# More zero products in TensorE's opening waits and a new order of the first 640 steps of a fused attention and gated-MLP kernel

## The chip, the cores and the metric

One core of one Trainium2 chip. The metric is the device time of one execution in microseconds, as the median of several runs. A profile is one further execution; its span runs from the first to the last instruction of the program.

## What is computed

Eight batches of attention with eight heads of 576 positions and 64 channels, in a causal window of 128 positions with a linear bias for each head; then, on the joined heads (576 by 512), a gated MLP whose gate mixes positions.

```python
scores = scale * q @ k.T + bias          # masked to 0 <= i - j < 128
x = softmax(scores) @ v                  # heads side by side: 576 x 512
h = gelu(x @ w_in)                       # 576 x 1024
u, v = h[:, :512], h[:, 512:]
v_n = (v - mean(v)) / sqrt(var(v) + 1e-6) * g_ln
gated = u * (w_sg @ v_n + b_sg[:, None])
out = x + gated @ w_out
```

All inputs and outputs are float32.

## The kernel before, in words

Attention is done for pairs of heads: 32 pairs, numbered 0 to 31, four to a batch. The MLP follows for each batch, its products split into a high and a low part (three products for one). The weights come from memory as float32 in 64-bit words and are split on the chip, which is work of the opening alone: the eight blocks of w_in must be split ahead of the first u product.

The kernel is a list of named steps. Each step belongs to one engine and issues a few instructions. The text `ORDER` (from L1150) holds all steps in one written-out order, and the loop at L1232 issues them so; each engine runs its own steps strictly in that order, and the engines are held together by semaphores alone. A step is named by a letter and a number. The steps of pair n (`Pair.STEPS`, table `add_pair`):

- q, L: loads of q and k, and of v, on SyncE's queue (SP). Each engine's DMA steps stand in one queue, so a load that waits for a free buffer holds up those behind it.
- a, c (and * for both): the scores on TensorE (PE), L278, 20 and 16 products.
- A, B, C, G: bias, mask and row minima on VectorE (DVE), L302 and L295. They free the PSUM banks of the scores.
- e, E, f, F, j: the exponentials on ScalarE (ACT), L311.
- R: the inverse of the sums, DVE, L322 and L323.
- s, S, r: the scaling, on ACT (L329) and GpSimd (POOL, L334).
- t, T, z: transposes on PE, L347 and L360; X, Y: the masked copies on DVE, L356; P: a copy on ACT, L363.
- V: the weighted values on PE, L384 (36 products) and L388 (4); x, p on ACT and 2 on DVE (L396) join them. So "20", "21", "22", "23" are step 2 of pairs 0 to 3.
- h on ACT and l on POOL: the high and low parts of the pair's output (L401, L218).

Pairs 0, 1, 3, 2 come first in this order. The splitting of weight block k is i (load, L181), d (ACT, L192 and L194), b (DVE, L196), o (DVE, L198), + (POOL, L218), H (ACT, L203) and - (DVE, L208, for odd k; POOL, L218, for even k). wl, wH, w- do it for the mixing weights. The four staging buffers of i and wl are shared: each later load waits until + of an earlier block has given one free.

Of the first batch's MLP, w and v on PE (L607 to L609) build the v half pair by pair: w20 is block 2 of positions from pair 0, and v0t closes block t with pair 2, the last. u000 is the first product group of the u half. vg is the gelu of v on ACT (L786).

A step Wi issues so many products of a zeroed tile, named `spare`, as the list `IDLE` says, into a PSUM bank of the named pool (L1139); nobody reads them. It needs the zeroed tile (L90) and a free buffer of that pool: two pools, ps_s and ps_a, have two one-bank buffers each, and ps_m has two of two banks.

Of the kernel before, what the change touches and what calls it, by code (L numbers as in the profile page):

```python
# [21 lines left out]
def attention_gmlp(  # L22
# [1123 lines left out]
    for b in range(B):  # L1146
# [14 lines left out]
        nv30h P4 bH nt0c vn03 b- vn02 V4 nt0h x4 d8 p4 uc01 tn0 b11 o11 b8 24 o8 y020 y021 *7 +11 ug0 A7 +8 B7 y000
        y001 H11 j7 H8 Us0 C7 G7 -11 -8 Us1 gm02 gm00 F7 E7 f7 e7 q9 q6 L6 *6 A6 R7 gh00 gh02 h4 B6 C6 e6 q8 L7 s7
        y010 y011 t7 S7 gl02 r7 T7 y030 G6 gm01 X7 F6 E6 f6 j6 R6 gl00 s6 S6 Y7 y031 z7 gm03 gh01 h5 P7 V7 p7 gh03
        gl01 t6 T6 X6 Y6 Oa0 x7 gl03 r6 O00 z6 27 oa00 Us2 l4 l5 P6 h7 V6 p6 x6 Us3 26 O01 h6 l6 l7 *8 oa01 A8 B8 C8
        Us4 G8 u100 u101 e8 *9 E8 f8 j8 F8 R8 A9 B9 u110 s8 S8 r8 t8 C9 k4 k7 Uh1 uc10 E9 j9 f9 e9 k5 k6 Ul1 X8 G9
# [105 lines left out]
```

## Time and profile before

| what | value |
|---|---|
| median of 3 runs | 577.91 us (577.79 to 578.27) |
| span of the profiled execution | 577.4 us |
| median less span | 0.5 us |
| instructions | 14654 |
| PE busy | 560.8 us, 97% of the span |
| DVE busy | 473.8 us, 82% |
| ACT busy | 378.6 us, 66% |
| POOL busy | 308.0 us, 53% |

For the profiled execution only its span is shown, so sums are made against 577.4 us, and 0.5 us is added for the median of the runs. The page gives one execution: the busy time of each engine, the chain of work that ended last, and the costliest groups of instructions. The trace behind it gives windows of time, timelines and waits. The granted clock is TensorE's alone, as a share of 2.4 GHz; ahead of its first record (at 14.2 us here) the windows show 1.00, and the products' durations have to tell.

### The profile page before, as it was taken

To read this page: it belongs to the slowest core of one execution; us is meant where nothing else is said; L and a number is where in the kernel's file an instruction comes from. 1 tells how busy PE (TensorE), PEld (TensorE's weight loads), DVE (VectorE), ACT (ScalarE), POOL (GpSimd) and SP (SyncE) were. 2 spreads that over 40 slices of the span, in tenths; PEclk is the share of its full clock that TensorE was granted. 3 is DMA by queue.
4 is the path that set the end of the run, shared out by engine and by line. 5 is a ranking of instruction groups with operands and counts; after the bars stand their busy time and mean duration, and the time that the engine had idled before them with its cause. 6 is when DMAs were issued, how large, how long until landed. Compare 5 with 4: busy or idle time off the path is not lost.

```text
span 577.4 us, 14654 instructions
## 1 busy us (share of the span) xinstructions
PE 560.8 (97%) x5495; PEld 512.7 (89%) x5495; DVE 473.8 (82%) x1324; ACT 378.6 (66%) x1063; POOL 308.0 (53%) x365
## 2 busy tenths in 40 slices
PE   5889999999999999999999999999999999999997
PEld 4667899998899799997999998998989999998997
DVE  7989998799989868899788987878897988666646
ACT  7988997466853867467776576746695667833422
POOL 3676646530436543575447753496347653576325
PEclk9989999999999999999999999999999999999999
DMA  8675213216403413454260465135332606012502
GB/s 297 190 235 199 72 45 121 69 46 243 167 37 125 156 37 99 146 192 129 60 212 10 140 204 173 43 103 168 130 120 65 214 2 197 2 35 96 171 1 82
DMA packets 43561, 69.78 MB, mean 121 GB/s; under 512 B 3554, under 2 KB 31202, under 8 KB 43492
## 3 DMA queue, kind: packets, MB, share of 16 engines
q1 hardware_dynamic: 43492, 68.86, 36.7%
q8 instruction: 43, 0.70, 0.5%
q14 instruction: 26, 0.21, 0.1%
HBM read 56.27 MB, written 12.58 MB: 119 GB/s over the span
## 4 chain that ended last, share of the span: by engine, by line
PE 90%; DVE 5%; DMA 2%; ACT 1%; issue 1%; POOL 0%; SPq 0%; DVEq 0%; ACTq 0%
PE ps_m L607 13%; PE ps_m L1059 13%; PE ps_m L609 12%; PE ps_m L608 12%; PE ps_m L905 12%; PE ps_a L347 5%; PE ps_s L384 4%; PE ps_s L278 4%; PE ps_a L278 4%; PE ps_m L384 3%; DMA qk<-qkT 2%; PE ps_m L941 2%; PE ps_m L940 1%; DVE px L356 1%; DVE e L295 1%; PE ps_m L796 1%
## 5 line engine op out<-in xcount | busy, mean ns | idle before, releaser
L334 POOL TENSOR_TENSOR e<-e,rr 128x256 f32<-128x256 f32 (+2 forms) x116 | 80.7, 718 | 97.0 <-DVE rr L323 84.9
L311 ACT ACTIVATE e<-e,stats 128x128 f32<-128x128 f32 (+1 forms) x288 | 110.6, 386 | 17.7 <-DVE stats L295 17.1
L224 POOL TENSOR_TENSOR region<-u,region 128x288 fp32r<-128x288 f32 (+1 forms) x78 | 77.7, 1016 | 44.7 <-ACT region L1006 16.2
L356 DVE TENSOR_TENSOR px<-ps_a,m_both 128x1024 f32<-128x1024 f32 x64 | 77.4, 1216 | 5.9 <-PE ps_a L347 5.4
L607 PE MATMUL ps_m<-ws,region 128*128 128x288 f32 x256 | 78.2, 306 | 0.0
L609 PE MATMUL ps_m<-ws,region 128*128 128x288 f32 x256 | 75.7, 296 | 0.0
L608 PE MATMUL ps_m<-ws,region 128*128 128x288 f32 x256 | 75.6, 295 | 0.0
L730 POOL TENSOR_TENSOR rs<-rs,mhalf 128x1 f32<-128x1 f32 (+1 forms) x40 | 30.2, 756 | 57.4 <-DVE rs L727 57.2
L218 POOL TENSOR_TENSOR xs<-xf,xs 128x288 fp32r<-128x288 f32 (+1 forms) x48 | 49.9, 1060 | 13.8 <-ACT xs L401 13.8
L311 ACT ACTIVATION_READ_ACCUMULATOR e<-e,stats 128x1 f32 x288 | 54.4, 189 | 0.0
L1006 ACT ACTIVATE region<-u 128x576 fp32r<-128x576 f32 x35 | 23.7, 684 | 43.4 <-PE ps_m L608 17.4
L607 PEld LDWEIGHTS ps_m<-ws,region 128*128 128x128 f32 x256 | 48.3, 189 | 1.5 <-issue 0.8
L608 PEld LDWEIGHTS ps_m<-ws,region 128*128 128x128 f32 x256 | 48.2, 188 | 0.1
L609 PEld LDWEIGHTS ps_m<-ws,region 128*128 128x128 f32 x256 | 48.1, 188 | 0.1
L607 PE MATMUL ps_m<-wi,xs 128*128 128x512 f32 x112 | 46.9, 418 | 0.1
L1066 DVE TENSOR_TENSOR xf<-ps_m,xf 128x576 f32<-128x576 f32 x48 | 35.7, 750 | 10.9 <-PE ps_m L1059 10.1
L609 PE MATMUL ps_m<-wi,xs 128*128 128x512 f32 x112 | 44.3, 395 | 0.0
L608 PE MATMUL ps_m<-wi,xs 128*128 128x512 f32 x112 | 44.2, 395 | 0.0
L946 DVE TENSOR_TENSOR u<-ps_m,u 128x576 f32<-128x576 f32 x32 | 24.0, 752 | 18.7 <-PE ps_m L941 11.5
L347 PE MATMUL ps_a<-ident,e 128*128 128x128 f32 x256 | 38.0, 275 | 1.0 <-DVE px L356 1.0
L295 DVE CUSTOM_DVE_ANT_0 e<-ps_s,bias 128x128 f32<-128x128 f32 (+1 forms) x140 | 34.9, 287 | 2.5
L278 PE MATMUL ps_s<-qk 64*64 64x192 f32 (+2 forms) x576 | 31.5, 333 | 5.3 <-DMA qk<-qkT 4.9
(217 smaller groups left out, 1600.9 us busy)
## 6 DMA issues: line engine op xcount, KB each, us to landing
qk<-qkT SPq DMA_DIRECT2D x32, 576.0 KB, 4.7
sum<-store SPq DMA_DIRECT2D x36, 512.0 KB, 4.8
outT<-xf SPq DMA_DIRECT2D x31, 288.0 KB, 3.0
vt<-v_in SPq DMA_DIRECT2D x32, 256.0 KB, 4.1
wst<-w_in SPq DMA_DIRECT2D x8, 512.0 KB, 4.8
store<-sum SPq DMA_DIRECT2D x6, 512.0 KB, 2.7
vt<-v_in SPq DMA_DIRECT2D x64, 32.0 KB, 4.2
wst<-w_out SPq DMA_DIRECT2D x4, 512.0 KB, 3.6
```

Of the source, the lines that this page charges most:

```text
L218: (engine or nc.gpsimd).tensor_tensor(out[:, cs], a[:, cs], b[:, cs], op)
L224: nc.gpsimd.tensor_tensor(out[:, fs], a[:, fs], b[:, fs], ALU.subtract)
L278: return lambda: nc.tensor.matmul(banks[half][to, c:c + k1 - k0], qk[js, 0, q0:q0 + R], qk[js, 1, k0:k1], start=True, stop=True)
L311: nc.scalar.activation(x, x, AF.Exp, bias=self.nm[0:n, i:i + 1], scale=-1.0, accum_out=self.sm[0:n, i:i + 1])
L334: nc.gpsimd.tensor_tensor(x[:, z:z + step, :], y[:, z:z + step, :], self.rr[0:n, i + z:i + z + min(k, step)].rearrange("p (m o) -> p m o", ...
L347: burst([lambda t=t: nc.tensor.transpose(cv[:, t // 2, t % 2], self.pr[j][:, t, :].rearrange("p (h c) -> p h c", h=2), ident[:, j * R:j * ...
L356: nc.vector.tensor_tensor(xv, cv, mv, ALU.mult)
L607: nc.tensor.matmul(dst, ah, bh, start=(first and i == 0), stop=False)
L608: nc.tensor.matmul(dst, ah, bl, start=False, stop=False)
L609: nc.tensor.matmul(dst, al, bh, start=False, stop=(last and i == n - 1))
L905: nc.tensor.matmul(dst, left(n, g, c)[:, ms], right(n, h, c), start=first and c == 0 and k == 0, stop=c == 1 and k == 2, skip_group_check= ...
L1059: nc.tensor.matmul(dst, p, q, start=first and f == 0 and k == 0, stop=f == 1 and k == 2, skip_group_check=True)
```

## The change

The list of the zero products becomes longer (24 entries with 85 products, where there were 12 with 51), and the steps of all engines up to some 640 of 2003 stand in a new order. No step is added or taken out but W steps, and from step gh15 on, in the MLP of the second batch, the order is the same. Two of the W steps, W7 and W11, now stand ahead of the first scores a0. On PE the last W step is now W22, ahead of t3; before, four stood behind t3 (W10 and W6, then W7 ahead of z3, and W1 ahead of u000).

```diff
-    IDLE = [(12, "ps_a"), (4, "ps_a"), (4, "ps_s"), (4, "ps_s"), (4, "ps_a"), (4, "ps_m"), (4, "ps_m"), (3, "ps_m"), (4, "ps_m"), (4, "ps_m"), (2, "ps_m"), (2, "ps_m")]
+    IDLE = [(4, "ps_m"), (4, "ps_m"), (5, "ps_m"), (1, "ps_m"), (4, "ps_a"), (4, "ps_a"), (4, "ps_a"), (4, "ps_a"), (4, "ps_a"), (5, "ps_a"), (2, "ps_m"), (1, "ps_m"), (4, "ps_m"), (4, "ps_m"), (2, "ps_m"), (3, "ps_m"), (4, "ps_m"), (3, "ps_m"), (3, "ps_a"), (4, "ps_a"), (5, "ps_a"), (5, "ps_s"), (4, "ps_s"), (2, "ps_s")]
...
-        q0 i2 d2 i1 q1 a0 c0 A0 a1 i0 B0 C0 G0 b2 c1 e0 d1 E0 F0 j0 f0 d0 b1 o2 o1 +2 A1 R0 B1 C1 b0 o0 G1 L0 i5 q3 i3
-        j1 H2 s0 E1 e1 f1 r0 F1 d3 S0 +0 +1 -2 W0 t0 X0 W5 T0 Y0 W2 W4 z0 R1 b3 o3 P0 r1 V0 z1 H0 p0 s1 H1 x0 a3 A3 B3
-        t1 20 X1 c3 C3 G3 -0 +3 S1 T1 W9 wl2 wH2 P1 w-2 i6 q2 d5 d6 H3 h0 wl3 L1 i7 q5 L2 F3 j3 e3 E3 f3 d7 a2 b5 b6
-        o5 +5 l0 Y1 A2 B2 R3 o6 -3 -1 b7 W11 W8 W3 V1 s3 w20 t3 W10 W6 x1 p1 j2 e2 21 h1 +6 S3 X3 c2 l1 w30 T3 W7 w00
-        w21 E2 wH3 C2 f2 G2 F2 r3 z3 w-3 H6 P3 Y3 R2 s2 -6 o7 S2 +7 L3 i9 i4 gb i10 V3 x3 23 p3 k1 H5 r2 h3 w01 t2 w10
-        T2 X2 Y2 l3 w31 w11 z2 d4 d10 P2 V2 x2 H7 p2 b4 o4 b10 o10 22 +4 +10 w13 w33 *5 A5 B5 C5 G5 w03 w23 h2 H4 d9
-        l2 v03 v02 v00 v01 W1 e5 j5 vg03 H10 vg02 vg00 vg01 -5 b9 o9 -7 -4 nv30b nv00b nv10b -10 +9 nv00p u000 u030
...
+        W7 q0 W11 i2 d2 a0 c0 A0 B0 W21 C0 G0 e0 b2 q1 i1 a1 A1 j0 E0 c1 L0 f0 B1 F0 R0 d1 i0 W6 i3 j1 W9 s0 W13 S0 r0
+        o2 +2 b1 o1 +1 W4 q2 q3 d0 C1 W8 W20 f1 G1 F1 t0 W5 W0 X0 T0 Y0 E1 W15 b0 o0 +0 W12 W1 z0 e1 R1 P0 i5 W10 d3 b3
+        o3 W23 i6 V0 W16 r1 z1 a3 L1 x0 wl2 +3 20 p0 W17 A3 B3 W3 s1 t1 H0 S1 gb X1 c3 -0 C3 G3 T1 h0 l0 W2 i7 L2 d6 d5
+        b5 o5 Y1 b6 W14 a2 A2 B2 w20 w30 e3 wH2 E3 w-2 H1 wl3 -1 W18 P1 d7 j3 V1 f3 w00 W19 b7 o7 F3 R3 e2 j2 x1 o6 W22
+        21 s3 p1 t3 X3 +5 c2 r3 E2 +7 C2 S3 T3 h1 G2 Y3 +6 w10 wH3 H2 z3 l1 w11 f2 F2 P3 -2 R2 q5 H3 -3 L3 V3 w-3 s2 S2
+        w01 t2 i10 x3 23 i4 H6 -6 r2 p3 w31 h3 i9 X2 l3 T2 Y2 d10 b10 d4 w21 z2 P2 d9 V2 tl o10 w33 b4 x2 o4 +4 b9 22 H7
+        -7 p2 h2 l2 +10 H4 H5 w23 k1 *5 L5 w03 A5 o9 v03 B5 v00 e5 C5 v02 vg00 -4 wl0 vg03 G5 vg02 k2 w13 v01 +9 -5 u000
...
```

## Rows read from the trace of the kernel before

**Rows 1.** The page: busy time of each engine, and the chain that ended last.

```profile
PE 560.8 (97%) x5495; PEld 512.7 (89%) x5495; DVE 473.8 (82%) x1324; ACT 378.6 (66%) x1063; POOL 308.0 (53%) x365
...
PE 90%; DVE 5%; DMA 2%; ACT 1%; issue 1%; POOL 0%; SPq 0%; DVEq 0%; ACTq 0%
```

**Rows 2.** Windows: stretch, length, each engine's busy time (instructions), granted clock, DMA share, GB/s.

```profile
6.50:31.21 24.71, 18.89 (x204) 14.28 (x196) 22.84 (x99) 23.98 (x87) 14.03 (x11) 1.00 0.80 256
...
28.40:31.26 2.86, 1.41 (x9) 0.98 (x8) 2.68 (x14) 2.82 (x15) 2.66 (x2) 1.00 0.88 305
...
31.29:34.71 3.42, 3.42 (x41) 2.96 (x42) 3.39 (x6) 2.83 (x9) 2.54 (x2) 0.50 0.36 108
...
56.98:160.00 103.02, 103.02 (x1065) 93.34 (x1069) 93.36 (x278) 76.47 (x220) 47.10 (x48) 1.00 0.32 107
```

The engines stand in the order PE, PEld (weight loads), DVE, ACT, POOL.

**Rows 3.** Timeline of PE in the opening: start, duration, line, operation, tiles, shape, count [idle before].

```profile
4.86 1.56 PE L278 MATMUL ps_s<-qk 64*64 64x128 f32 x20 [4.86 <-DMA qk<-qkT]
...
9.64 1.56 PE L278 MATMUL ps_m<-qk 64*64 64x128 f32 x20 [1.94 <-DMA qk<-qkT]
...
12.41 2.66 PE L1139 MATMUL ps_a<-spare 128*128 128x288 f32 x12
...
21.00 0.88 PE L278 MATMUL ps_s<-qk 64*64 64x128 f32 x20
...
31.26 2.88 PE L384 MATMUL ps_s<-px,vt 64*64 64x128 f32 x36
...
34.28 0.68 PE L607 MATMUL ps_m<-wi,xs 128*128 128x512 f32 x1
...
35.27 0.60 PE L347 MATMUL ps_a<-ident,e 128*128 128x128 f32 x4
35.62 1.36 PE L1139 MATMUL ps_m<-spare 128*128 128x288 f32 x6
...
41.30 1.57 PE L384 MATMUL ps_s<-px,vt 64*64 64x128 f32 x36
...
55.85 0.69 PE L1139 MATMUL ps_a<-spare 128*128 128x288 f32 x4
56.98 0.40 PE L607 MATMUL ps_m<-xs,wi 128*128 128x288 f32 x1 [0.43 <-ACT xf L786]
```

**Rows 4.** Timeline of DVE in the opening, with the same columns.

```profile
18.68 1.03 DVE L322 TENSOR_SCALAR rr<-stats 128x9 f32<-128x9 f32 x1
...
21.97 0.30 DVE L302 COPY_PREDICATED ps_s<-sel,ps_s 128x128 f32<-128x128 uint8 x1 [1.00 <-PE ps_s L278]
...
31.12 0.17 DVE L322 TENSOR_SCALAR rr<-stats 128x9 f32<-128x9 f32 x1
...
34.31 1.26 DVE L196 TENSOR_SCALAR tmp<-tmp 128x512 int32<-128x512 int32 x1
...
37.83 0.30 DVE L302 COPY_PREDICATED ps_s<-sel,ps_s 128x128 f32<-128x128 uint8 x1 [0.54 <-PE ps_s L278]
...
43.41 0.69 DVE L396 TENSOR_TENSOR xf<-ps_s,xf 128x512 f32<-128x512 f32 x1 [1.97 <-ACT xf L393]
...
46.62 0.42 DVE L196 TENSOR_SCALAR tmp<-tmp 128x512 int32<-128x512 int32 x1
47.07 0.69 DVE L198 SCALAR_TENSOR_TENSOR tmp<-wst,tmp 128x512 int32<-128x512 int32 x1
...
48.14 1.67 DVE L198 SCALAR_TENSOR_TENSOR tmp<-wst,tmp 128x512 int32<-128x512 int32 x1
49.73 0.68 DVE L396 TENSOR_TENSOR xf<-ps_s,xf 128x512 f32<-128x512 f32 x1
```

**Rows 5.** Timeline of POOL in the opening, with the same columns.

```profile
33.80 1.49 POOL L334 TENSOR_TENSOR e<-e,rr 128x512 f32<-128x512 f32 x1
...
47.90 1.36 POOL L218 TENSOR_TENSOR tmp<-tmp,wst 128x512 int32<-128x512 int32 x1 [1.41 <-ACT p L363]
```

More of the change, by code (lines that the diff above doesn't have):

```diff
@@ L1161, in attention_gmlp @@
[L1161 to L1165, printed above, removed]
@@ new lines, in attention_gmlp @@
+        nt1c D00 r9 nt1p u110 q11 V8 x8 p8 nt1h t9 X9 28 u120 Us9 T9 Y9 u111 tn1 z9 P9 u121 Uh3 L9 uc12 Ul3 ks0 ks1 ks2
+        ks3 uc11 V9 p9 x9 ks4 29 kh0 kl0 ks5 ug1 ks6 kh1 kl1 O03 oa03 q10 O02 oa02 D02 *10 A10 B10 C10 G10 E10 f10 e10
+        j10 F10 v10 *11 A11 vg10 L10 v11 R10 r10 s10 vg11 t10 B11 C11 nv01b nv01c nv01p nv01h nv11b nv11p nv11c v12 vn10
+        nv11h X10 vn11 vg12 v13 ya100 ya101 vg13 kh2 nv21b nv21c S10 q12 nv21p nv21h T10 E11 G11 ya110 z10 nv31b nv31p
+        Y10 P10 ya111 nv31c nv31h vn12 vn13 kl2 ks7 ks8 V10 y110 f11 y111 gm11 j11 e11 ks9 x10 q13 D03 F11 kh3 R11 s11
@@ new lines, in attention_gmlp @@
+        y100 y101 gm10 kl3 kd0 y120 y121 y130 h9 t11 gh11 gl11 gt11 210 h8 p10 y131 l9 kd1 gm12 gh15 X11 gm13 O11 S11
+        gl15 r11 gt12 T11 z11 O15 h10 gh12 gh16 gh13 P11 Y11 oa11 gl12 V11 x11 p11 gl16 gt13 O16 211 gh17 oa15 oa16 gt14
+        *13 gl13 O13 gl17 ut25 oa13 O17 A13 oa17 O12 B13 oa12 h11 gh14 gl14 l8 O14 C13 oa14 G13 l10 l11 E13 k10 uh25 k9
+        k11 k8 v20 v21 vg20 ul25 vg21 j13 ut26 ut27 nv02b nv02c nv02p nv02h nv12b nv12p nv12c nv12h vn20 vn21 *12 tt2
+        U21 kd2 lu21 lu22 q14 lu20 L12 D11 D10 q15 L13 tj2 U25 uh27 f13 uh26 e13 ue21 A12 B12 ut24 ul27 ul26 U26 F13
@@ new lines, in attention_gmlp @@
+        ue25 U23 uh24 E12 ue26 U27 C12 ue23 G12 R13 e12 f12 j12 F12 U22 ue27 R12 ul24 U24 ue22 r12 s12 z12 t12 S12 tg2
+        nt2b nt2p s13 X12 nt2c ue24 v22 T12 Y12 v23 vg22 nv22b P12 nt2h tn2 vg23 V12 p12 x12 nv32b nv32c 212 nv22c nv22p
+        nv32p S13 h12 l12 r13 ug2 nv22h nv32h ya200 ya210 *14 A14 B14 vn22 ya201 t13 ya211 z13 vn23 y200 y201 X13 gm20
+        C14 y210 y211 y220 T13 gm21 G14 E14 P13 f14 gh21 j14 F14 e14 Y13 gl21 y221 *15 y230 R14 A15 gt21 B15 gm22 C15
+        r14 s14 S14 y231 gh25 f15 gm23 gl25 gt23 gt22 z14 t14 V13 E15 gh23 P14 p13 x13 gh27 O21 gh22 j15 X14 213 lo21
@@ new lines, in attention_gmlp @@
+        A18 B18 nv13b ut34 ul36 U36 r17 s17 t17 z17 ue35 uh34 ue36 C18 nv13c U33 ue33 X17 S17 nv03p nv13p ul34 U37 U32
+        ue37 T17 U34 nv13h P17 j18 E18 f18 vn31 ue32 G18 nv03c Y17 nv03h ue34 p16 F18 e18 vn30 v33 D22 R18 *19 vg33 V17
+        x17 ug3 A19 s18 B19 C19 nv33b 217 nv33c v32 t18 ya310 vg32 E19 nv23b nv23c r18 S18 nv33p nv23p j19 ya300 ya301
+        z18 ya311 X18 nv23h nv33h p17 vn32 vn33 e19 h17 G19 h16 P18 F19 l17 k17 f19 lo32 L19 L18 lo31 q20 q21 lo30 T18
+        y310 Y18 y300 y301 *20 gm30 R19 A20 V18 B20 x18 r19 s19 S19 z19 y311 t19 P19 T19 218 C20 gm31 G20 X19 y320 y321
@@ new lines, in attention_gmlp @@
+        y330 y331 gh31 j20 E20 p18 h18 gl31 l16 gm32 gt31 e20 F20 f20 k16 gh35 l18 Y19 gm33 gl35 gt32 R20 gt33 *21 A21
+        V19 gh33 x19 O31 gl33 r20 s20 z20 219 gh37 gh36 gh32 P20 O35 t20 oa31 gl36 O36 oa35 B21 C21 oa36 gl32 gt34 gl37
+        O33 O37 oa33 S20 T20 O32 p19 ut45 h19 j21 E21 gh34 k18 f21 oa37 X20 oa32 gl34 O34 l19 uh45 e21 k19 tt4 G21 Y20
+        F21 oa34 tj4 ul45 R21 ut46 tg4 q22 D31 *22 nt4b s21 nt4p S21 L20 D30 D33 D32 V20 x20 nt4c uh46 nt4h lu41 lu40
+        q25 q23 lu42 L21 220 v41 v40 A22 vg41 B22 ut47 uh47 tn4 vg40 r21 z21 U41 t21 U45 ul47 ul46 E22 ue41 U46 C22
@@ new lines, in attention_gmlp @@
+        nv04b nv14b f22 P21 j22 ue45 U43 X21 ut44 G22 nv04c e22 ue46 nv14p ue43 nv14c F22 uh44 p20 ul44 U47 T21 R22 ue47
+        Y21 U42 U44 ue42 *23 A23 ue44 B23 V21 r22 nv04p s22 S22 nv04h nv14h x21 C23 f23 j23 221 vn41 E23 vn40 v42 z22
+        v43 t22 vg42 nv24b P22 G23 nv24c vg43 nv24p p21 h20 nv24h ug4 nv34b nv34p nv34c vn42 nv34h h21 e23 F23 T22 ya410
+        ya400 ya401 ya411 L22 q24 lo41 L23 lo42 lo40 vn43 y410 y400 y411 y401 X22 Y22 gm41 R23 *24 gm40 A24 B24 V22 x22
+        gh41 C24 f24 j24 e24 r23 s23 S23 l20 gl41 t23 X23 222 T23 y420 E24 p22 z23 y421 y430 y431 Y23 gt41 G24 F24 P23
@@ new lines, in attention_gmlp @@
+        gh45 gm42 R24 gm43 *25 V23 s24 l21 gl45 S24 O41 A25 gt43 gt42 B25 gh43 x23 k20 j25 h22 gh46 p23 gl43 223 gh42
+        oa41 gl46 t24 T24 O45 C25 oa45 O46 oa46 O43 gl42 gt44 oa43 k21 gh47 gh44 E25 gl47 l22 k22 h23 f25 O47 O42 X24
+        oa47 G25 oa42 gl44 r24 l23 O44 oa44 ut55 k23 z24 tt5 F25 v51 Y24 P24 uh55 e25 tj5 R25 tg5 nt5b ut57 q29 q26 *26
+        nt5c L24 lu50 D40 D41 L25 lu51 q27 D43 lu52 V24 s25 ul55 ut56 A26 vg51 x24 uh57 nt5p nt5h uh56 ul57 ul56 224 tn5
+        v50 vg50 t25 U51 U55 nv05b ut54 B26 nv05c ue51 U56 ue55 uh54 ue56 p24 r25 z25 U53 C26 X25 ue53 U57 ul54 S25
@@ new lines, in attention_gmlp @@
+        nv05p G26 ue57 T25 j26 f26 U52 P25 nv05h U54 F26 ue54 e26 Y25 nv15b nv15p ue52 *27 V25 A27 vn50 x25 E26 B27
+        nv15c nv15h 225 C27 vn51 R26 v53 vg53 ug5 r26 s26 v52 G27 nv35b nv35c S26 nv35p vg52 nv25b nv25p nv25c t26 z26
+        ya510 ya500 X26 ya511 ya501 T26 f27 j27 nv25h vn52 nv35h e27 p25 vn53 h25 P26 F27 E27 y510 y511 Y26 lo52 L27
+        lo50 q28 D42 lo51 L26 *28 gm51 A28 R27 V26 l25 s27 S27 r27 B28 e28 x26 h24 l24 p26 E28 y500 C28 226 G28 y501 t27
+        gm50 F28 gh51 f28 X27 T27 j28 y520 z27 y521 y530 y531 gl51 k25 h26 P27 gm52 gt51 R28 gh55 Y27 gm53 l26 s28 gl55
@@ new lines, in attention_gmlp @@
+        gh53 gl53 r28 S28 *29 gt53 gt52 A29 V27 gh56 x27 O51 gh57 B29 j29 E29 e29 p27 gh52 k26 227 oa51 gl56 C29 z28 t28
+        O55 oa55 O56 X28 oa56 O53 gl52 gt54 gl57 T28 oa53 O57 O52 Y28 oa57 G29 oa52 L28 q31 L29 lu60 q30 D51 lu62 lu61
+        D50 f29 gh54 gl54 O54 P28 h27 l27 k27 k24 ut65 F29 uh65 tt6 oa54 R29 ut67 tj6 *30 V28 tg6 x28 nt6b A30 228 nt6c
+        B30 ul65 s29 r29 nt6p S29 v61 z29 v60 vg61 nt6h uh67 ul67 ut66 tn6 nv16b C30 uh66 vg60 ul66 nv16p U61 t29 X29
+        U65 T29 j30 ue61 p28 U66 E30 ue65 U63 ut64 ue66 e30 U67 Y29 nv06b G30 nv16c F30 uh64 f30 P29 ue63 U62 ue67 R30
@@ new lines, in attention_gmlp @@
+        ue62 *31 A31 s30 ul64 S30 r30 nv06p B31 V29 nv16h j31 E31 x29 C31 229 t30 U64 T30 v63 X30 nv06c ue64 nv06h p29
+        e31 lo62 lo61 L31 L30 D52 D53 lo60 vn60 Y30 vn61 G31 z30 v62 vg63 nv36b vg62 nv26b nv26c nv36c P30 nv26p nv36p
+        F31 f31 ya610 V30 p30 nv26h nv36h ug6 ya600 ya601 ya611 vn62 R31 vn63 y600 y601 s31 y610 r31 h28 l28 z31 t31
+        y611 gm60 h29 x30 y620 l29 S31 y621 gm61 230 X31 gh61 gl61 gt61 T31 Y31 gm62 y630 y631 gm63 h30 gh65 k29 gh63
+        gt63 gl65 O61 gt62 O65 gh67 P31 V31 gh66 k28 p31 gh62 x31 oa61 gl66 oa65 O66 gl63 gl67 gl62 oa66 231 O63 oa63
```

84 lines of the change are left out of this document (19 added, 65 removed).

## The prediction

> **What bounds the kernel now.** I read the page first. TensorE (PE) is busy for 97% of the span, and the chain that ended last lies on PE for 90% of it [rows 1]. So the time is the moment from which PE never waits, plus the work that then remains. The windows show that moment [rows 2]: from 56.98 us on, PE is busy for all of 103.02 us, while in the opening before it PE has holes and VectorE (DVE) and ScalarE are nearly full. The row at 56.98 us is the first product of u000 [rows 3]. All that the change can win or lose is how early u000 starts; behind it the same products remain, and PE has nothing left to give there.
>
> Next I followed PE through the opening [rows 3]. Three things stand out. First, the scores of the first two pairs run at half speed: 20 products took 1.56 us at 4.86 and at 9.64, and the same 20 took 0.88 us at 21.00. The zeros at 12.41 start at the slow rate too. Second, the granted clock is 0.50, which is 1.2 instead of 2.4 GHz, from 31.29 to 34.71 us [rows 2]; V1, the weighted values of pair 1, falls into it: its 36 products took 2.88 us, those of V3 1.57 us. PE had been busy for only half of the stretch ahead of it, 1.41 of 2.86 us [rows 2]. Third, V1 itself starts only when the minima of pair 2 (B2) have given its PSUM banks free; the next step's first operation starts at 31.12 as B2's last result is written, at about 31.2 [rows 4]. DVE is therefore what holds the opening: 22.84 us busy of the 24.71 us up to that point [rows 2].
>
> Last I looked at why DVE is slow where it is slow [rows 4]. Its weight-splitting operations take 0.42 us (L196) and 0.69 us (L198) when GpSimd (POOL) is idle. Where a product of POOL had started before (at 33.80 and 47.90 [rows 5]), they took 1.26 and 1.67 us; and the 128x9 operation at L322 took 1.03 instead of 0.17 us. Each such meeting cost DVE 0.84 to 0.98 us.
>
> **The change part by part.** *Zeros ahead of the first scores.* W7 and W11, five products, need only the zeroed tile. At the slow rate (12 products in 2.66 us [rows 3]) they take 1.2 us and are over before the first q and k land at about 4.8 us, so they delay nothing. If the clock were up by then, a0 would end up to 0.7 us earlier (1.56 less 0.88); a loss is excluded, as PE waits for the DMA anyway. In the kernel before, PE worked on from 9.64 to 14 us before its products became fast, so I take 0. Their cover is the DMA; without it they would cost 1.2 us.
>
> *q1 is issued ahead of i1.* a1 waited 1.94 us for q1 [rows 3]. W21 and a1 now fill this hole. A1 moves from 11.66 to about 10.5 us, but DVE's work up to B2 is a closed list, so this is worth only what DVE does not then wait elsewhere. The other moved loads (i0, i5, L0, gb) land well ahead of their users; if the queue stood still behind i5, which now waits for +2, d5 would be the first to be late, with some 4 us in hand. I take 0.
>
> *The 26 zeros between c1 and t0* cost some 3 us of PE (half of the 0.22 us each that W0's twelve took at the slow rate [rows 3]). X0 on DVE stands behind C1 and G1, so t0 has that long; cover is DVE. Likewise the 23 zeros between t0 and V0, behind Y0.
>
> *DVE up to the end of B2.* Both orders run the same steps. The new one drops three delays of the old: R1's meeting (0.86), a small one of R0 (0.2) and the wait of 1.00 us for a3's scores. It adds about 0.45 us for a1 (W21 stands before it). And it brings new meetings with POOL: o2, b1 and o1 now follow R0, whose result also starts S0 and whose o2 starts +2. So b1 stands behind S0 and o1 behind +2; these two follow from the order alone. b3 behind +0 and o5 behind w-2 depend on the instant. At 0.9 us each (mean of the rows above), from 24.71 us: with none 23.1, with two 24.9, with three 25.8, with four 26.7 us. Followed step by step with all four, and with ScalarE's d3 waited for, B2 ends as late as 34.2 us, 3.0 later than now; with none it ends at 29.6, 1.6 earlier. I take three meetings, the two sure ones and one of the others: B2 1.1 us later.
>
> The Trainium skill, page "SBUF — State Buffer", section "Who interferes with whom", says that whichever of the two engines starts first holds their shared port for its whole instruction and the other blocks fully. The rows agree: 1.26 for 0.42 us. By that rule every meeting is paid in full, which is the first rival below.
>
> *PE from V1 to u000.* Now 25.7 us (31.26 to 56.98). Taken out: w20 and w30, moved ahead of V1 (0.99 us from 34.28 to 35.27, and some 0.8); W10 and W6 (1.36), W7 (half of that, 0.7) and W1 with the wait behind it (1.13); V1's slow rate (1.4). Put in: the eight zeros of W19 and W22, some 1.4 us by the row of six. That leaves 20.7 us, 5.0 less, if PE alone counted.
>
> *DVE from B2 to u000.* It does not: DVE's own steps up to "22" are 13.7 us at the durations above, against 19.2 us now (31.21 to 50.41). What goes: the wait of 0.54 us for c2 (zeros stood ahead of it), part of the 1.97 us for x3 [rows 4], and V1's slow rate. What stays: -1, o6 and R2 still meet POOL, and 22 still waits for x2. Followed step by step this comes to 16.8 us, 2.4 less, and from 22 to u000 0.7 less, as W1 is gone. Next in line is then l2 on POOL, then the gelu of vg. So B2 to u000 is 3.1 us shorter; the ends are 0 and PE's 5.0.
>
> *Sum:* +1.1 - 3.1 = -2.0 us for u000. Behind it DVE is busy for 93.36 of 103.02 us [rows 2], so a tenth of a microsecond may be lost again: -1.9. The profiled execution's span of 577.4 us becomes 575.5; the median of the runs is 577.9, 0.5 above that span, so I say 576.0 us.
>
> **The rivals.** *All meetings are paid* (no change). For it: the rows, in which POOL's head start was paid every time. Against: in two of four places POOL's product may be over or not yet begun. B2 at 34.2, then 3.1 us won back: -0.2, 577.7 us.
>
> *The clock falls again ahead of V1* (slower). Between w30 and V1 only the three zeros of W18 stand. If B2 is late, PE has nothing from about 31 to 34 us, longer than the half-idle stretch of 2.86 us that now ends in the fall. V1 and w00 then run at 1.2 GHz: 1.4 and 0.2 us, and x1, 21 and all behind them wait for that. Against: w20 and w30 now stand in that hole. It decides once B2 ends later than about 33 us. -0.2 + 1.6 = +1.4, 579.3 us.
>
> *No meeting at all:* B2 at 29.6 and 3.1 us won: -4.7, 573.2 us. Against it speak b1 and o1.
>
> *The zeros do nothing:* the clock rises where it did and falls where it did. The opening's early part doesn't mind, since DVE sets it; V1's 1.6 us would stay, and the forecast would be 577.6. I count it with no change.
>
> **How the numbers follow.** 0.2% of the time, 1.16 us, is about what a measurement here can tell from no change. The forecast (two or three meetings) has 0.33 and no meeting 0.14: faster 0.47. All paid, or zeros without use: same 0.28. The clock's second fall, with what else a late V1 drags along: slower 0.25. The likeliest single case is 576.0, and its own range, two to four meetings, is 575.0 to 577.0. For 8 in 10 the range must reach to the other cases: from 573.4, nearly no meeting, to 579.5, the second fall.
>
> **What would show it.** Right: u000's first product at about 55 us; V1 at 31 to 33 us at full clock; w20 and w30 ahead of it; b1 and o1 long, 1.3 to 1.7 us. Wrong: a granted clock of 0.50 in the stretch around V1; B2 ending past 33 us; u000 behind a wait for l2 or for the gelu; or holes of PE behind u000, where now there are none, which would mean that DVE no longer keeps up and that the whole sum looks at the wrong place.

## The result, and the profile after

The kernel after takes 581.91 us (median of 5 runs, 579.49 to 582.0), the kernel before 578.05 us beside it (577.79 to 578.51). The ratio is 1.0058, with an interval of 1.0046 to 1.0069: the change is slower, by 3.9 us. The forecast was 576.0.

The page of the kernel after, its busy times and the chain that ended last, to be set against [rows 1]:

```profile
PE 566.0 (98%) x5529; PEld 517.4 (89%) x5529; DVE 477.4 (82%) x1324; ACT 379.5 (65%) x1063; POOL 313.0 (54%) x365
...
PE 82%; DVE 9%; ACT 4%; DMA 1%; issue 1%; POOL 0%; SPq 0%; DVEq 0%; POOLq 0%
```

PE's share of the chain fell from 90% to 82% and DVE's rose from 5% to 9%: the stretch in which DVE sets the pace has probably become longer. The windows say which stretch (columns as in [rows 2]):

```profile
6.50:33.51 27.01, 23.13 (x248) 18.57 (x240) 26.03 (x99) 25.12 (x90) 13.13 (x10) 0.99 0.77 258
30.52:33.56 3.04, 1.10 (x7) 0.66 (x7) 2.86 (x15) 3.04 (x15) 0.95 (x1) 0.93 0.84 291
33.11:39.94 6.83, 6.45 (x51) 5.51 (x50) 4.56 (x11) 4.60 (x19) 4.18 (x4) 0.50 0.25 69
59.02:160.00 100.98, 100.31 (x1036) 90.68 (x1035) 92.23 (x276) 74.15 (x211) 48.65 (x46) 1.00 0.36 119
```

Up to the end of B2 there are the same 99 DVE instructions as in [rows 2], but 27.01 us instead of 24.71: DVE's busy time grew by 3.19 us and its idle time fell by 0.89. Just ahead of V1, PE is busy for 1.10 of 3.04 us. Then the granted clock is 0.50 (1.2 GHz) for 6.83 us, twice as long as before. Behind u000, PE is no longer full: 0.67 us are missing.

Why DVE is late stands in its timeline (columns as in [rows 4]); the rows are b1, o1, b3, o5, and then X3, which waits for t3:

```profile
12.66 1.27 DVE L196 TENSOR_SCALAR tmp<-tmp 128x512 int32<-128x512 int32 x1
13.96 1.69 DVE L198 SCALAR_TENSOR_TENSOR tmp<-wst,tmp 128x512 int32<-128x512 int32 x1
...
20.77 1.43 DVE L196 TENSOR_SCALAR tmp<-tmp 128x512 int32<-128x512 int32 x1
...
28.30 1.79 DVE L198 SCALAR_TENSOR_TENSOR tmp<-wst,tmp 128x512 int32<-128x512 int32 x1
...
40.37 1.23 DVE L356 TENSOR_TENSOR px<-ps_a,m_both 128x1024 f32<-128x1024 f32 x1 [2.63 <-PE ps_a L347]
```

And POOL's timeline beside them (columns as in [rows 5]), S0, +2, +0 and w-2:

```profile
12.36 1.29 POOL L334 TENSOR_TENSOR e<-e,rr 128x512 f32<-128x512 f32 x1 [8.98 <-ACT e L311]
13.61 1.49 POOL L218 TENSOR_TENSOR tmp<-tmp,wst 128x512 int32<-128x512 int32 x1
...
20.62 1.29 POOL L218 TENSOR_TENSOR tmp<-tmp,wst 128x512 int32<-128x512 int32 x1 [3.52 <-DVE rr L322]
...
27.98 1.56 POOL L218 TENSOR_TENSOR ws<-wst,ws 128x576 fp32r<-128x576 f32 x1
```

Each of the four DVE rows begins 0.15 to 0.35 us after a POOL row and ends 0.3 to 0.55 us behind its end. Against 0.42 and 0.69 us [rows 4] they lost 0.85, 1.00, 1.01 and 1.10 us, 3.96 together; what the new order drops, R1's meeting of 0.86 us above all [rows 4], takes part of it back. All four meetings that the prediction named were paid. The rule it quoted from the Trainium skill ("SBUF — State Buffer", section "Who interferes with whom"), that the later engine waits for the whole of the other's instruction, agrees with all four.

PE's timeline around V1 (columns as in [rows 3]): W18, V1 in two parts, w00, W19, W22, t3, and far behind them u000 and z7:

```profile
31.28 0.67 PE L1139 MATMUL ps_a<-spare 128*128 128x288 f32 x3 [0.77 <-DVE px L356]
32.75 0.44 PE L384 MATMUL ps_s<-px,vt 64*64 64x128 f32 x4 [0.80 <-PE ps_a L1139]
33.56 2.61 PE L384 MATMUL ps_s<-px,vt 64*64 64x192 f32 x32 [0.38 <-DVE stats L295]
...
36.17 0.79 PE L607 MATMUL ps_m<-wi,xs 128*128 128x512 f32 x1
...
37.62 1.16 PE L1139 MATMUL ps_a<-spare 128*128 128x288 f32 x4
38.58 1.16 PE L1139 MATMUL ps_s<-spare 128*128 128x288 f32 x4
39.54 0.80 PE L347 MATMUL ps_a<-ident,e 128*128 128x128 f32 x4
...
59.02 0.30 PE L607 MATMUL ps_m<-xs,wi 128*128 128x288 f32 x1
...
95.01 0.33 PE L360 MATMUL ps_a<-ident,e 128*128 128x128 f32 x1 [0.67 <-POOL e L334]
```

V1's main part starts as B2 ends and runs at half speed; so do w00 and the eight zeros of W19 and W22. t3 starts at 39.54 instead of 35.27 us.

So the loss is read from three stretches, and every run below is read by the same three: when B2 ends, from there to u000's first product, and from there to the end of V7 (the weighted values of pair 7). For before they are 31.21, 25.77 and 43.62 us, for after 33.51, 25.51 and 44.41: +2.30, -0.26 and +0.79, which is the 2.8 us between the two spans (577.4 and 580.2).

The medians differ by 1.1 us more. In every execution whose span is listed, the time is 1.65 to 2.3 us above the span. The profiled execution of before, 577.4 us of span, was therefore well above the median: of 88 further executions of it, 59 had a span of 576.5 us or less and four had more than 577.4.

### The profile page after: what moved, and what is told of

Its sections match the earlier page's. It is cut to its first block, busy times and chain, and to the rows that moved or that the text cites. A ratio compares the mean times of both kernels' runs of the same rounds, so it can differ in the third digit from the quotient of the medians.

```text
span 580.2 us, 14726 instructions
## 1 busy us (share of the span) xinstructions
PE 566.0 (98%) x5529; PEld 517.4 (89%) x5529; DVE 477.4 (82%) x1324; ACT 379.5 (65%) x1063; POOL 313.0 (54%) x365
## 4 chain that ended last, share of the span: by engine, by line
PE 82%; DVE 9%; ACT 4%; DMA 1%; issue 1%; POOL 0%; SPq 0%; DVEq 0%; POOLq 0%
PE ps_m L1059 13%; PE ps_m L905 12%; PE ps_m L607 11%; PE ps_m L609 11%; PE ps_m L608 11%; PE ps_a L347 4%; PE ps_m L384 3%; PE ps_a L278 3%; PE ps_s L384 3%; PE ps_s L278 3%; DVE e L295 2%; DMA qk<-qkT 1%; PE ps_m L941 1%; PE ps_m L940 1%; DVE tmp L198 1%
## 5 line engine op out<-in xcount | busy, mean ns | idle before, releaser
L334 POOL TENSOR_TENSOR e<-e,rr 128x256 f32<-128x256 f32 (+2 forms) x116 | 82.3, 734 | 108.3 <-DVE rr L323 90.2
L218 POOL TENSOR_TENSOR xs<-xf,xs 128x288 fp32r<-128x288 f32 (+1 forms) x48 | 51.1, 1087 | 11.0 <-ACT xs L401 11.0
L1059 PE MATMUL ps_m<-region,sum 128*128 128x288 f32 x252 | 36.5, 298 | 0.0
## 6 DMA issues: line engine op xcount, KB each, us to landing
qk<-qkT SPq DMA_DIRECT2D x32, 576.0 KB, 4.6
```

The lines of the kernel that those rows point to most:

```text
L218: (engine or nc.gpsimd).tensor_tensor(out[:, cs], a[:, cs], b[:, cs], op)
L334: nc.gpsimd.tensor_tensor(x[:, z:z + step, :], y[:, z:z + step, :], self.rr[0:n, i + z:i + z + min(k, step)].rearrange("p (m o) -> p m o", ...
L1059: nc.tensor.matmul(dst, p, q, start=first and f == 0 and k == 0, stop=f == 1 and k == 2, skip_group_check=True)
```

## The experiments

The theories: **order** (the meetings make B2 late), **clock** (PE's empty stretch ahead of V1 lets the clock fall, and the fall costs), **zeros** (the added products stand on the path). The table has all runs: B2's end and the two stretches from one profile each, the median of the time, and its ratio to before on the same chip. A profile is one execution and need not be the median one. e5 is the kernel before, built once more: its median lay 0.6 us above that of before in the same session, so a difference of that size between two kernels says little. A W step's number is its place in the kernel's `IDLE` and differs between kernels; in the diffs of e4, e6 and e8 the W steps and `IDLE` keep the numbers and the order of the kernel that was edited.

| run | B2 ends | to u000 | u000 to V7 | time | ratio (95% interval) |
|---|---|---|---|---|---|
| before | 31.21 | 25.77 | 43.62 | 578.05 | |
| after | 33.51 | 25.51 | 44.41 | 581.91 | 1.0058 (1.0046 to 1.0069) |
| e1 old order, new zeros | 32.89 | 25.27 | 43.64 | 578.68 | 1.0016 (1.0008 to 1.0025) |
| e2 new order, old zeros | 35.31 | 23.79 | 44.41 | 582.92 | 1.0084 (1.0070 to 1.0098) |
| e3 no zeros before t3 | 33.55 | 24.98 | 44.40 | 580.68 | 1.0048 (1.0035 to 1.0060) |
| e4 more zeros before V1 | 33.68 | 23.18 | 44.41 | 580.44 | 1.0038 (1.0024 to 1.0052) |
| e5 before again | 31.73 | 25.09 | 43.62 | 578.69 | 1.0005 (0.9995 to 1.0015) |
| e6 fewer meetings | 30.84 | 23.19 | 44.42 | 577.48 | 0.9986 (0.9977 to 0.9995) |
| e7 e4 with z7 later | 33.47 | 23.17 | 44.32 | 580.15 | 1.0029 (1.0018 to 1.0040) |
| e8 before, more zeros | 31.06 | 25.07 | 43.65 | 578.44 | 1.0002 (0.9994 to 1.0011) |
| e9 before, with meetings | 36.38 | 25.07 | 43.64 | 583.28 | 1.0092 (1.0078 to 1.0106) |
| e10 e6 without W19, W22 | 30.77 | 23.17 | 44.41 | 577.73 | 0.9995 (0.9986 to 1.0004) |
| e11 e6, old tail | 31.42 | 23.18 | 47.23 | 579.07 | 1.0017 (1.0008 to 1.0025) |
| e12 old opening, new tail | 31.17 | 25.07 | 44.52 | 579.26 | 1.0022 (1.0013 to 1.0031) |
| f1 e9 with the new zeros | 34.01 | 24.93 | 43.63 | 581.43 | 1.0062 (1.0048 to 1.0075) |
| f2 e6, old order behind V4 | 30.54 | 23.16 | 43.63 | 575.62 | 0.9954 (0.9941 to 0.9966) |

**e1 and e2: order and zeros apart.** The old order with the new zeros (where no bank was free, two W steps went in with a neighbour; 26 zeros between c1 and t0, as in the change):

```diff
-+0 +1 -2 W0 t0 X0 W5 T0 Y0 W2 W4 z0
++0 +1 -2 W3 W4 W5 W6 W7 W8 t0 X0 W9 W10 T0 Y0 W11 W12 W13 z0
...
-b7 W11 W8 W3 V1 s3 w20 t3 W10 W6 x1
+b7 W20 V1 s3 w20 W21 t3 x1
```

> The order of before with the 85 zero products of the change at the same neighbours on TensorE. If the order alone makes the change slow (GpSimd meets VectorE at b1, o1, b3 and o5, so that B2 ends 2.3 us later), this stays within 1 us of the kernel before (577.5 to 578.5 us), B2 still ends at about 31.2 us and V1 starts there. If the zeros make it slow (8 of them ahead of t3 on the path, 1 to 2 us), it is at 579 to 580.5 us. If the clock is kept up by zeros and each fall costs some 2.4 us, it may be as fast as 575.5 to 576.5 us in the executions in which the granted clock stays at 1.00.

And the new order with the old zeros:

```diff
-j3 V1 f3 w00 W19 b7 o7 F3 R3 e2 j2 x1 o6 W22
-21 s3 p1 t3 X3 +5 c2
+j3 W5 W6 W7 V1 f3 w00 b7 o7 F3 R3 e2 j2 x1 o6
+21 s3 p1 t3 X3 +5 W8 W9 c2
```

> The order of the change with the 51 zero products of before at the same neighbours. If the order alone makes the change slow, this is at 580 to 582.5 us, with B2 ending at 33 us or later. If the zeros are the cause (the eight ahead of t3), it is at 577.5 to 579.5 us. The ten zeros ahead of V1, in place of three, then stand in TensorE's empty stretch from 30.5 us; if they keep the clock at 1.00 around V1, the time is at 579 to 580 us even though B2 is late.

Measured: 578.68 and 582.92 us, each a little above what was expected for that case. The order is the cause: with either set of zeros it costs 3.2 to 5.0 us. The zeros pull both ways. In the new order the new ones are worth 1.0 us (582.92 to 581.91). In the opening they go with a clock that stays up until V1; in e2, with the old ones, it fell much earlier (window of that fall):

```profile
14.57:24.81 10.24, 8.41 (x73) 6.61 (x72) 7.96 (x20) 6.81 (x27) 4.87 (x5) 0.50 0.66 206
```

B2 ended at 35.31 us there, 1.80 later than in the change, and V1 ran at full speed, behind ten zeros. In the old order the new zeros seem to cost about 0.7 us, not clearly more than e5's 0.6. e1's profile shows how they can: the 26 zeros are not covered there. X0 waited 0.54 us for t0, and the scores of pair 3, behind more zeros, came 2.83 us after DVE was ready for them. But it is the slowest of e1's eleven executions (580.31 us), so that a B2 as late as 32.89 is not its usual one.

**e3 and e4: the zeros on the path, and the clock.** W19 and W22 taken out:

```diff
-j3 V1 f3 w00 W19 b7 o7 F3 R3 e2 j2 x1 o6 W22
+j3 V1 f3 w00 b7 o7 F3 R3 e2 j2 x1 o6
```

> The change without W19 and W22, the eight zero products between w00 and t3. If they stand on the path (they took 1.92 us at half clock, and t3's scaled exponentials were done 0.4 us after the first of them began), t3, X3 and all behind come 1.0 to 1.9 us earlier: 580.0 to 581.0 us. If t3 is late because s3 on ScalarE stands behind x1, which waits for V1, only some 0.4 to 1.5 us of that comes back. If the order up to B2 alone is the cause and DVE's lateness is made up anyway, nothing changes: 581.5 to 582.0 us.

W18 made longer:

```diff
-(4, "ps_m"), (3, "ps_m"), (3, "ps_a"), (4, "ps_a"),
+(4, "ps_m"), (3, "ps_m"), (14, "ps_a"), (4, "ps_a"),
```

> The change with 14 zero products in place of 3 as W18, in TensorE's empty stretch between w30 and V1 (30.5 to 33.5 us). If the fall of the granted clock at 33.1 us costs what the one execution without a fall shows (577.7 us of span against some 580.1), and more zeros prevent the fall, the time is at 579.3 to 579.8 us with a granted clock of 1.00 around V1 and B2 unchanged at 33.5 us. If the clock falls for another reason than the empty stretch, it falls again and the time is 581.5 to 582.5 us. If the late B2 alone sets the time, 581.9 us at either clock.

PE's timeline of e4 ahead of V1, and its windows for PE's formerly empty stretch and for B2 to u000:

```profile
31.46 2.11 PE L1139 MATMUL ps_a<-spare 128*128 128x288 f32 x14 [0.76 <-DVE px L356]
33.50 1.65 PE L384 MATMUL ps_s<-px,vt 64*64 64x128 f32 x36
```

```profile
30.52:33.56 3.04, 2.28 (x17) 1.94 (x17) 2.86 (x13) 3.02 (x16) 1.12 (x1) 1.00 0.86 291
33.68:56.86 23.18, 22.06 (x241) 16.60 (x239) 22.52 (x57) 21.13 (x59) 18.89 (x14) 1.00 0.50 161
```

With PE busy for 2.28 instead of 1.10 us of the 3.04, the clock stayed up, V1 took 1.65 us, and B2 to u000 was 23.18 us instead of 25.51. The fall costs 2.33 us there. The time is only 1.5 us lower, and at 580.44 above the 579.3 to 579.8 expected: behind V7 the profile of e4 takes 477.4 us, that of after 476.8. B2 is as late as ever. In e3 the clock fell again (mean 0.994 in the profile), t3 came 1.9 us earlier, but only 0.53 us of it reached u000. So the eight zeros are a quarter of the fall's price. e3's median is 1.2 us below the change's, but three of its five executions had a mean clock of 0.999 or 1.000, so that part of this is the clock's.

**e5 and e8: was the fall in the kernel before worth anything?** The kernel before once more, unchanged:

> The kernel before, unchanged, for a profile of an execution without a fall of the clock: most executions of it show a mean granted clock of 1.000 and a span of about 576.1 us, where the profile shown has a fall at 31.29 us and a span of 577.4 us. If that fall is what the profiled execution alone paid, V1 takes 1.6 instead of 2.9 us here, u000 starts at some 55.8 us instead of 56.98, and the span is 576.0 to 576.3 us. If the fall is hidden behind VectorE, u000 starts at 57 us all the same.

And with ten more zeros ahead of V1:

```diff
-(4, "ps_m"), (4, "ps_m"), (2, "ps_m"), (2, "ps_m")
+(4, "ps_m"), (9, "ps_m"), (2, "ps_m"), (7, "ps_m")
```

> The kernel before with ten more zero products between a2 and V1 (W11 7 instead of 2, W8 9 instead of 4), in the empty stretch ahead of V1. If the fall in the profiled execution stood for all executions, this is worth its price, some 1.2 us: 576.5 to 577.0 us. If most executions of before have no fall, the median moves by less than 0.3 us: 577.6 to 578.0 us, with a granted clock of 1.000 in all of them.

e5 missed: its span was 577.3, with a fall at another place, and B2 ended 0.52 us later. From the window of that fall, and PE's row for V1:

```profile
11.18:14.59 3.41, 3.41 (x37) 2.67 (x29) 3.17 (x18) 3.41 (x16) 2.51 (x2) 0.50 0.91 324
```

```profile
31.79 1.57 PE L384 MATMUL ps_s<-px,vt 64*64 64x128 f32 x36
```

Still it gives the price: with V1 at full speed, B2 to u000 is 25.09 us in e5 and 25.07 in e8 (whose fall lay at 25.44 to 28.85) and e12, against 25.77 with V1 at half speed [rows 3]. In the old order the fall at V1 cost 0.7 us, not the 1.4 of V1's own length. e8 missed too: its median (578.44 us) is not below that of before, and six of its eleven executions had a mean clock of 0.996 or 0.997. In its profile V1 ran at full speed and the fall lay elsewhere.

**e6: the meetings taken out of the change.** o2 and +2 go ahead of A1, b1 and o1 behind G1:

```diff
-e0 b2 q1 i1
+e0 b2 o2 +2 q1 i1
...
-S0 r0 o2 +2 b1 o1 +1 W4 q2
+S0 r0 W4 q2
...
-f1 G1 F1
+f1 G1 b1 o1 +1 F1
```

> The change with o2 and GpSimd's +2 ahead of A1, where VectorE reads PSUM, and b1, o1 behind G1, so that S0 runs beside C1 and G1; the meetings of b1 and o1 should be gone (0.42 and 0.69 instead of 1.27 and 1.69 us). If the meetings are the cause of the late B2, B2 ends 1.2 to 1.9 us earlier, at 31.6 to 32.3 us, and the time is 1 to 2 us less than the change: 580 to 581 us with a fall of the clock, 576.5 to 578.5 us in executions without one. If VectorE then only waits longer for the scores of pair 3, B2 moves by less than 0.5 us and the time stays at 581.5 to 582 us.

DVE's timeline of e6 (C1's first two operations, and then b1 and o1), and its POOL row for S0:

```profile
12.88 0.28 DVE L302 COPY_PREDICATED ps_s<-sel,ps_s 128x128 f32<-128x128 uint8 x1
13.19 0.29 DVE L295 CUSTOM_DVE_ANT_0 e<-ps_s,bias 128x128 f32<-128x128 f32 x1
...
14.37 0.42 DVE L196 TENSOR_SCALAR tmp<-tmp 128x512 int32<-128x512 int32 x1
14.83 0.69 DVE L198 SCALAR_TENSOR_TENSOR tmp<-wst,tmp 128x512 int32<-128x512 int32 x1
```

```profile
13.11 1.04 POOL L334 TENSOR_TENSOR e<-e,rr 128x512 f32<-128x512 f32 x1 [0.78 <-DVE rr L323]
```

```profile
6.50:30.84 24.34, 22.74 (x248) 19.06 (x240) 22.39 (x99) 23.51 (x83) 13.27 (x10) 1.00 0.79 261
30.84:54.03 23.19, 21.99 (x236) 16.60 (x237) 22.53 (x58) 22.61 (x68) 18.89 (x14) 1.00 0.58 184
```

S0 now runs beside C1, whose operations read the scores from PSUM and take their usual 0.28 and 0.29 us. The Trainium skill (the same section) says that a VectorE instruction with at most one input in SBUF, outside its two-port modes, doesn't contend with GpSimd; the rows agree. b3 and o5 moved off their meetings too (0.43 and 0.69 us), so all four are gone: DVE's busy time up to B2 falls by 3.64 us against the change, B2 ends 2.67 us earlier (1.2 to 1.9 were expected), and the clock stays up with W18's three zeros as they were. Part of the gain is given back in a wait for ScalarE's d3, ahead of b3:

```profile
20.15 0.43 DVE L196 TENSOR_SCALAR tmp<-tmp 128x512 int32<-128x512 int32 x1 [0.88 <-ACT tmp L194]
```

Moving five steps takes 4.4 us off: 577.48 us, 0.6 below the kernel before, which is no more than e5's distance from it.

**e9 and f1: the meetings put into the kernel before.** e9 has this edit alone (s0 and S0 move with it), f1 has it and the zeros of e1:

```diff
-f0 d0 b1 o2 o1 +2 A1 R0 B1 C1 b0
+f0 d0 A1 R0 s0 S0 o2 +2 b1 o1 B1 C1 b0
```

> The kernel before with o2, b1 and o1 moved behind R0 and S0 (as the change has them), nothing else moved but s0 and +2 with them. If the meetings of b1 with S0 and of o1 with +2 are the cause, b1 takes some 1.27 and o1 some 1.69 us here too; the wait of 1.00 us for a3's scores takes up part of the 1.85 us, so that B2 ends 0.9 to 1.9 us later than in the kernel before, and the time rises by 1 to 2 us (579 to 580 us), more where the clock falls around V1. If the meetings don't matter for the time, it stays within 0.5 us of the kernel before.

> The kernel before with the two meetings put in (583.28 us without more zeros, clock down from 19.94 to 26.76 us), now with the zero products of the change at the same neighbours. If the fall of the clock made most of that loss, the clock stays at 1.00 up to V1, a3's scores take 0.88 instead of 1.41 us, B2 ends 1 to 2 us later than in the old order with these zeros (32.89 us) and the time is 579.5 to 581 us. If the meetings themselves and what stands behind them on VectorE make the loss, the time stays above 582 us.

Both have b1 at 1.27 and o1 at 1.68 us. e9 lost far more than expected: B2 at 36.38. Its windows, its V0 on PE, and A3 on DVE say why:

```profile
13.00:20.00 7.00, 3.65 (x27) 3.18 (x25) 6.83 (x20) 5.70 (x25) 3.74 (x4) 1.00 0.37 126
20.00:27.00 7.00, 6.50 (x67) 5.37 (x67) 3.53 (x6) 3.81 (x11) 5.38 (x5) 0.52 0.64 204
```

```profile
22.21 2.88 PE L384 MATMUL ps_m<-px,vt 64*64 64x128 f32 x36
```

```profile
27.13 0.30 DVE L302 COPY_PREDICATED ps_s<-sel,ps_s 128x128 f32<-128x128 uint8 x1 [3.53 <-PE ps_s L278]
```

With DVE late, PE had nothing to do for half of 13 to 20 us; the clock fell, V0 and a3 ran at half speed, and DVE in its turn waited 3.53 us for a3's scores. With the zeros of the change in those holes (f1) the clock stayed at 1.00, A3 came 2.36 us earlier, and so did B2. So of the 4.65 us by which e9's B2 is later than e5's, half goes with the clock, and the other 2.28 us stay without any fall. The two meetings of 1.85 us are not the whole of these: A1, now ahead of b1, waits for a1's scores (0.87 us in e9), and f1's zeros may delay B2 as those of e1 did. f1's time, 581.43 us, is a little above the 579.5 to 581 expected.

**e7: is z7 the loss behind u000?** The kernel is e4, with its 14 zeros as W18, and this edit:

```diff
-S7 F6 z7 P7 y011 gm01
+S7 F6 y011 z7 P7 gm01
```

> The change with the 14 zeros of W18 (which kept the clock at 1.00) and with z7 behind y011 on TensorE, so that r7 on GpSimd has a y group more of time. In the run with the 14 zeros TensorE waited 0.68 us for r7 at 92.85 us, where the kernel before never waited behind u000. If this hole is a loss of its own, the time is 0.5 to 0.7 us below the 580.44 us of that run: 579.7 to 579.95 us, and no hole over 0.3 us between 60 and 170 us. If it is made up later anyway, nothing changes (580.2 to 580.7 us).

The hole moved on. PE's timeline of e7, t6:

```profile
96.85 0.63 PE L347 MATMUL ps_a<-ident,e 128*128 128x128 f32 x4 [0.51 <-DVE rr L322]
```

580.15 against 580.44 us is within the scatter of both. z7 only showed the loss, it did not make it.

**e10: the eight zeros, without a fall.** e6 without W19 and W22 (the edit of e3):

> The change with the two meetings taken out (577.48 us), now without W19 and W22 too. If the eight zeros ahead of t3 are always on the path, this saves their 1.0 us at full clock: 576.3 to 576.8 us. If they were on the path only because V1 was late and the clock was down (in the mended run t3 started as s3 was done, and X3 behind step 21 on VectorE), nothing changes: 577.2 to 577.8 us. If they keep the clock up for what follows, it may even be slower, with a fall behind V1.

577.73 us, and 23.17 against 23.19 us from B2 to u000: at full clock the zeros are free.

**e11, e12 and f2: the order behind u000.** Three kernels that go over from one order to the other: e11 (from e6) and f2 (from e6) to the order of before, at u000 and at V4, and e12 (from the kernel before) to the new one, at u000. The first steps behind, in this order:

```diff
-u000 u001 H10 -10 nv00b nv00c nv00p vg01 nv10b nv10p u030
+u000 j5 H10 vg01 nv30b nv00b nv10b -10 nv00p u030
...
-P4 V4 bH nt0c nt0h p4 vn02 b- tn0 y020 b8 x4 24 b11 o11
+P4 V4 bH nt0c b- vn02 nt0h x4 p4 uc01 tn0 b11 o11 b8 24
...
-u000 u030 u001 F5 k0 H9
+u000 tl L5 wl0 k2 u001 nv00c nv10p u030 u031
```

> The change with the two meetings taken out, up to u000, and behind u000 the steps in the order of before. If the change loses 0.7 to 0.8 us behind u000 by its new order there (u000 to V7 takes 44.4 us in every run of the new order and 43.6 us in the old one, with a hole of 0.67 us at z7), this takes 576.5 to 576.9 us and has no hole of TensorE between 60 and 170 us. If the loss comes from what the new opening leaves undone, the hole stays or turns up elsewhere, and the time stays at 577.2 to 578 us.

> The kernel before up to u000, with its own zeros, and behind u000 the order of the change. If the new order behind u000 costs 0.7 to 0.8 us by itself, this takes 578.6 to 579.0 us, u000 starts where it did in the kernel before, and TensorE has a hole of some 0.7 us ahead of z7 or V7. If the new order there costs nothing without the new opening, it takes 577.8 to 578.3 us.

> The change with the two meetings taken out, up to V4, and the order of before behind it. V5 to V7 took 28.0 to 28.1 us in each run of the new order and 27.1 us in each run with the old one there. If the order of the steps there is the cause, the hole ahead of z7 is gone, V4 to V7 is 0.7 to 0.9 us shorter than in the mended run (21.98 us), and the time is 576.5 to 576.9 us, the fastest of all. If the hole comes from VectorE being late out of the new opening, it comes back at z7 or V7 and the time stays at 577.2 to 577.8 us.

e11 was no clean test: vg01, which the new order has behind u000 and the old one ahead of it, came too late, PE waited 2.12 us for a gelu (L786) at 58.49, and the clock fell. e12 is clear: the hole ahead of z7, 0.68 us, is there with the old opening too (PE's timeline):

```profile
92.35 0.33 PE L360 MATMUL ps_a<-ident,e 128*128 128x128 f32 x1 [0.68 <-POOL e L334]
```

f2 takes it away. Its window behind u000, where PE is full again:

```profile
53.70:160.00 106.30, 106.30 (x1108) 96.28 (x1107) 96.26 (x283) 79.41 (x232) 47.57 (x48) 1.00 0.33 114
```

The order behind V4 costs 0.8 us by itself. The rows point at Us2 and Us3, two sums over parts of w_in (L649). The new order has them ahead of R7, the old one behind V7; in the DVE timeline of after they are the last rows ahead of R7, for which POOL's r7, and behind it z7, then wait:

```profile
91.63 0.69 DVE L649 TENSOR_TENSOR sums<-sums 128x512 f32<-128x512 f32 x1
92.36 0.69 DVE L649 TENSOR_TENSOR sums<-sums,wi 128x512 f32<-128x512 f32 x1
92.97 0.17 DVE L322 TENSOR_SCALAR rr<-stats 128x9 f32<-128x9 f32 x1
```

No run moves these two alone. f2 takes 575.62 us, below the 576.5 to 576.9 expected, 1.9 below e6 and 0.46% below the kernel before: the fastest of all. Between the two profiles the span differs by 2.1 us: 0.3 ahead of u000, 0.8 up to V7 and 1.0 behind it. Of that last microsecond 0.6 is a wait of PE for a load of q and k, here in e6 and in f2, and 0.4 lies behind PE's last product (4.0 and 3.6 us to the end):

```profile
262.57 0.88 PE L278 MATMUL ps_a<-qk 64*64 64x128 f32 x20 [0.90 <-DMA qk<-qkT]
...
260.92 0.88 PE L278 MATMUL ps_a<-qk 64*64 64x128 f32 x20 [0.28 <-DMA qk<-qkT]
```

The same wait is 0.81 us in before and 0.38 in after, so it is not shown that f2's order shortened it.

## Why the prediction was wrong

**What held.** The bound in the opening: DVE's work up to B2 set V1 and with it most of the difference. The meetings: named, placed and priced right (0.85 to 1.10 us against 0.9). B2 to u000: forecast 22.7 us (25.77 less 3.1), and six runs of the new order in which the clock stayed up around V1 and W19 and W22 either ran at full clock or were gone, e4, e6, e7, e10, e11 and f2, measured 23.16 to 23.19. The zeros ahead of a0 and ahead of t0 cost nothing in the new order.

**The step that failed** is "I take three meetings", B2 1.1 us later. All four were paid, at 0.99 us each instead of 0.9, and B2 ended 2.30 us later: between the 2.0 that the prediction's own count gives for four (26.7 less 24.71) and the 3.0 that it had worked out step by step. Two of the meetings "depend on the instant", it said, and it counted one of the two.

**The second failure** weighs more in the sum: B2 to u000 was to become 3.1 us shorter and became 0.26 shorter, because the clock fell. The prediction had treated two rivals as different cases. "All meetings are paid" had B2 at 34.2 us, and "the clock falls again" decides "once B2 ends later than about 33 us": the first mostly brings the second, as the profile shows and as e9 and f1 show once more in the other order. Of the five executions of after, four had a fall and spans of 579.8 to 580.2 us; the one without had 577.7, which agrees with the price below. A late B2 with a quiet clock, which e4 made with eleven more zeros, took 580.44 us, not the 577.7 of the first rival. Taken as one case, with the 0.25 of the one and most of the 0.28 that the other shared with useless zeros, they would have been likelier than the forecast's 0.33, and on the slower side. The signs that it gave for being wrong at this place came: a clock of 0.50 around V1 and B2 past 33 us.

**Sizes.** (1) The rival of the fall came true, at 581.9 instead of 579.3 us. Its price was 2.33 us (e4 against after), not 1.6: the new order has x1 ahead of s3 on ACT, so V1's delay goes through x1 (2.71 us behind B2's end, 1.51 in e4) to s3, t3 and X3, and 0.53 us of it is W19 and W22, which the prediction priced at full clock. In the old order s3 stood ahead of x1, and the fall was half as long. (2) The gain of 1.4 us for "V1's slow rate" was in the old order worth 0.7. With a quiet clock the stretch from B2 to u000 became 2.6 us shorter (25.77 to 23.17) instead of 3.1: 0.7 for the old kernel's own fall, and 1.9 (25.08 to 23.17) by the new order itself. (3) Behind u000 "a tenth of a microsecond" was 0.8: DVE's busy share was the wrong witness, the order of the steps around V4 to V7 makes PE wait. The prediction named holes there as a sign of error, and they were; "all that the change can win or lose is how early u000 starts" does not hold. (4) "0.5 above that span" set the span of one execution against the median of others; the distance within an execution is 1.65 to 2.3, and 1.1 us of the difference of 3.9 lies there. (5) "No meeting at all", 573.2 us, is what e6 made, and it took 577.5: B2 ended at 30.84 us and not at 29.6, among others because DVE then waited 0.88 us for d3, which the count left out; the rest is (2), (3), (4) and the longer stretch behind V7.

**The sum as measured**, for after against before: B2 +2.3, its clock +2.3, the new order up to u000 -1.9 and the 0.7 that the profile of before had lost to its own fall, -0.7; behind u000 +0.8. That is +2.8 of span, and the profile of before, longer than its median execution, makes it 3.9.

**What stays open:** why the clock falls in one execution of a kernel and not in the next; whether Us2 and Us3 alone make the hole at z7; and whether f2's last microsecond belongs to its order. With both weak places mended the time is 575.62 us, 0.4 below the forecast. That is a coincidence: f2 has none of the four meetings, where the forecast counted three and the prediction had 573.2 for none.

## What to carry to other kernels

When an order is changed, list which SBUF operations of VectorE now run beside products of GpSimd, and place operations that read PSUM there instead: five moved steps were worth 4.4 us of 582. A late engine costs more than its lateness where TensorE runs dry behind it and loses its clock; so don't weigh "late" and "clock falls" as separate chances. And find out whether the profiled execution is a typical one before its span is taken as the base of a sum.
